# Attention, mixing MLP and gated output on one core: banks, copies and order of the first heads changed

## The chip, the cores and the metric

The kernel runs on one core of one Trainium2 chip. The metric is device microseconds of one execution, launch to end. A profiled execution also gives a trace. In it PE is the matrix engine (TensorE), DVE the vector engine, ACT the scalar engine, POOL GpSimd, SP the engine whose queue issues the DMAs here.

## What is computed

```python
# attn_out: 8 batches x 8 heads, 576 tokens, head size 64, block-causal mask (blocks of 64)
scores = scale * q @ k.T ; masked -> -1e9 ; p = exp(scores - max) ; p /= sum(p) + 1e-9
x = concat_heads(p @ v)                       # 8 x 576 x 512
h = x.T @ U @ V                               # mixing over tokens, rank 32
u = x + h.T
x = u + relu(u @ w_ch1) @ w_ch2               # 512 -> 2048 -> 512
gate = sigmoid(causal 5-tap convolution of x)
out = (gate * (x @ w_val)) @ w_out
```

U, V and the weights come as 64-bit floats; the kernel rebuilds single precision from their two words. Weights and most operands of the large products are split in a high and a low part, so that one product is three matmuls.

## The kernel before

**Stages.** A first stage runs the attention of batch 0 and of the first heads of batch 1 (ticks 0 to 11), with the mixing of batch 0, on an otherwise free PE. Then the MLP begins on groups of 512 tokens, sixteen steps each, and the remaining heads are cut in pieces that are dealt out between its matmuls (`gap`). At the end come the convolution, the gate and the last products.

**A tick.** `tick(n)` emits for head n the scores and for head e = n - 2 the values. For the first NQ = 18 heads (the early form) a tick has:

- two calls of `emit_q_bank`: each fills two PSUM banks with scores, one per head of the pair ("pS", from the pool `psum["a"]`), takes the row maxima on DVE ("rq", L415, and the negated maximum, L417 or L420) and the exponentials on ACT (L427, copies L425). Banks 0 and 1 of a pair come in the even tick, banks 2 and 3 in the odd one. All of it is at high priority.
- `mixing(2*e)`: steps of the token mixing of a pair of heads. In the first stage an even tick (from tick 4) has `mix_T`: PE turns the pair's normalised values `xt` ("pT", L646, L654), ACT and DVE split them. An odd tick (from tick 5) has `mix_G`: the product with U ("pG", L662), which goes by ACT (L664), DVE (L665), ACT (cast of g, L90) and DVE to `g`.
- `emit_pv(e, 0)` and `emit_pv(e, 1)`: the products of exponentials with values ("pPV", L586) for 128 and 448 tokens, each in a PSUM bank of `ps_p`; ACT copies the upper half of the bank to `xt` (L587) and the lower half, the sums of the exponentials, to `lt` (L588).
- `emit_est(e + 1)`, which for early heads is `emit_q_turn`: PE turns the exponentials of head e + 1 into four banks ("pE", L445), which ACT copies to the tile `e` (L446). It is at high priority.
- in an odd tick the normalisation of the pair: DVE turns `lt`, takes reciprocals, spreads them (L596 to L605), and POOL multiplies `xt` by them (L606).
- `mixing(2*e + 1)`: in an odd tick `mix_H`, the product with V ("pH", L685), the sum with `xt`, and the split into the MLP's `uh` and `ul`.

**What sets the order.** PE's instructions run in the order in which they are written. On the other engines a scheduler at build time orders by simulated readiness and by priority; each engine then works its queue in that order and waits at its head. In the first stage there are two PSUM pools of four banks: `ps_p`, from which pE, pPV, pT, pG and pH are taken in turn, and `psum["a"]`, from which pS is taken. A bank is taken again when the fourth allocation after it comes, and the writer waits until the earlier contents are read. From the first MLP step on both names are the same pool.

**Weights beside it.** Every twelfth `yield` of the stream in the first stage emits one conversion of a weight block (`conv`): a DMA of raw words, an absolute value on ACT ("wa", L119), four DVE operations (L121 to L142), a cast on ACT and a subtraction on POOL. The DMA of such a block is held back by a tiny DVE copy that reads the `xt` of the last emitted `emit_pv` (L553). After the first stage the remaining conversions are emitted two to a step, the first four together.

Of the kernel before, what the change touches and what calls it, by code (L numbers as in the profile page):

```python
# [8 lines left out]
F32 = mybir.dt.float32  # L9
# [8 lines left out]
P = 128  # L18
# [4 lines left out]
def attn_moe_gate_kernel(ctx: ExitStack, tc: tile.TileContext, q, k, v, U, V, w1, w2, wval, convw, wout, out):  # L23
    nc = tc.nc
    B, H, S, D = q.shape
# [46 lines left out]
    NQ = FIRST_SPLIT  # L72
# [14 lines left out]
    vec, act, pool, pe, sp = nc.vector, nc.scalar, nc.gpsimd, nc.tensor, nc.sync  # L87

    def hi_act(o, i):
        act.copy(o, i)  # L90
# [4 lines left out]
    def lo(eng, o, i, h):  # L95
        eng.tensor_tensor(o, i, f32(h), op=ALU.subtract)  # L96
# [63 lines left out]
    psum = {"a": first.enter_context(tc.tile_pool(name="ps0", bufs=8 - ABUF, space=PSUM, side="left"))}  # L160
# [39 lines left out]
    ps_p = att.enter_context(tc.tile_pool(name="psp", bufs=ABUF, space=PSUM, side="right"))  # L200
# [30 lines left out]
    def rot(tag, bufs=2, dtype=F32, n=S):  # L231
        return rot_p.tile([P, n], dtype, tag=tag, bufs=bufs, name=tag)
# [91 lines left out]
    def load_v(n):  # L324
        if not 0 <= n < NH:
            return
        vv = v[n // H, n % H]
        t = vstk[n % 2]
        sp.dma_start(out=t[:, 0:NK - 1, 0:D], in_=vv[0:S - D, :].rearrange("(i p) d -> p i d", p=P))
        sp.dma_start(out=t[D:P, NK - 1, 0:D], in_=vv[S - D:S, :])  # L330
# [3 lines left out]
    own = [slice(0, D), slice(D, P)]  # L334
# [13 lines left out]
    def kslice(j):  # L348
        return slice(q0[j], q0[j] + P) if q0[j] + P <= S else slice(S - P, S)
# [14 lines left out]
    def emit_s_piece(pn, i):  # L364
        heads = (2 * pn, 2 * pn + 1)
        if i == 0:
            for n in heads:
                stt[n] = [s_p.tile([P, w], F32, tag=f"s{h}", name=f"s{h}") for h, w in enumerate(sw)]
        todo, o = [], 0
        for j, a0, a1 in pieces[i]:  # L370
            todo.append((slice(a0, a1), kslice(j), o, True))
            o += a1 - a0
        j, a0, a1 = pieces[i][0]
        d = soff[j] + a0 - q0[j]
        for n, ps in zip(heads, beside(pn, todo)):
            act.copy(stt[n][half_of[j]][:, d:d + o], ps[:, 0:o])  # L376
# [54 lines left out]
    def emit_q_turn(n):  # L431

        eq = eqs.pop(n)
        for i, (half, c0, blocks) in enumerate(tbanks):
            if c0 == 0:
                e = e_p.tile([P, sw[half]], F32, tag=f"e{half}", name="e")
                est[n, half] = (e,)
            ps = ps_p.tile([P, 512], F32, tag="a", name="pE")
            o = c = D if i == 0 else 0
            todo = []  # L440
            for t, j in blocks:
                todo.append((t == NTT - 1, o if t < NTT - 1 else o - D, t, j))
                o += P if t < NTT - 1 else D
            for _, at, t, j in sorted(todo, key=lambda x: not x[0]):
                pe.transpose(ps[:, at:at + P], eq[t][:, kslice(j)], ident)  # L445
            act.copy(est[n, half][0][:, c0:c0 + o - c], ps[:, c:o])  # L446

    def emit_corners(n):
        for h, js in enumerate(((3, 0), (1, 2))):
            c0, c1 = (soff[j] // D for j in js)  # L450
            v_ = stt[n][h].rearrange("p (c w) -> p c w", w=D)
            pool.memset(v_[D:P, c0:c1 + 1:c1 - c0, :], MASKED)
        pool.memset(sv(n, NK - 1)[0:D], MASKED)
# [7 lines left out]
    def emit_max_a(n):  # L461
        m = rot("m", 1)
        vec.tensor_tensor(m[:, P:], sv(n, 0, P), sv(n, 1), op=ALU.max)
        for j in range(2, NK):
            x = vec.tensor_tensor(m[:, q0[j]:], m[:, q0[j]:], sv(n, j), op=ALU.max)
        noted(1, x)
        mxt[n] = m
# [30 lines left out]
    def emit_sub(n, half):  # L498
        mb = mbt[n]
        for j in parts[half]:  # L500
            noted(3, vec.tensor_tensor(sv(n, j), sv(n, j), mb[:, q0[j]:], op=ALU.subtract))  # L501
# [3 lines left out]
    def prep_v(n):  # L505

        if not FIRST_SPLIT <= n < NH:
            return
        t = vstk[n % 2]
        vlo[n] = late["v"].tile([P, NK, D], F32R, tag="vlo", name="vlo")  # L510
        if not vhi:
            vhi[0] = late["v"].tile([P, NK, P], F32R, tag="vhi", name="vhi")
            act.copy(vhi[0][:, :, D:P], t[:, :, D:P])
        v_, h_ = t[:, :, 0:D], vhi[0][:, :, 0:D]
        hi_act(h_, v_)
        lo(pool, vlo[n], v_, h_)
# [30 lines left out]
    last = [None]  # L547
# [7 lines left out]
    def emit_pv(n, c):  # L555
        b, h = divmod(n, H)
        pr, a = divmod(h, 2)
        if a == 0 and c == 0:
            xts[n // 2] = (late["x"] if n >= 3 * H and n // 2 % (NP + 2) == 0 else x_p).tile([P, S], F32, tag="xt", name="xt")
            lts[n // 2] = rot("lt", 1)  # L560
        xt, lt = xts[n // 2], lts[n // 2]
        last[0] = (own[a], xt[own[a]][0:1, 0:1])
        ps = ps_p.tile([P, 512], F32, tag="a", name="pPV")
        c0, c1 = ((0, P), (P, S))[c]
        split, whole = [], []
        for j in range(NK):
            a0 = max(c0, q0[j])
            if a0 >= c1:
                continue
            off = soff[j] - q0[j]  # L570
            rows = slice(0, P)
            o_, e_ = ps[:, a0 - c0:c1 - c0], slice(off + a0, off + c1)
            if n < FIRST_SPLIT:
                whole.append((o_, vstk[n % 2][rows, j, :], est[n, half_of[j]][0][rows, e_]))
            elif off + c1 <= WHOLE and half_of[j] == 0:
                whole.append((o_, vstk[n % 2][rows, j, :], est[n, 0][2][rows, e_]))
            else:
                eh, el, _, skip = est[n, half_of[j]]
                e_ = slice(off + a0 - skip, off + c1 - skip)
                for v_, m, t in ((vhi[0], P, eh), (vhi[0], P, el), (vlo[n], D, eh)):  # L580
                    split.append((o_[:m], v_[rows, j, 0:m], t[rows, e_]))
        todo = split + whole
        if len(todo) > 1:
            todo.append(todo.pop(1))
        for i, (o_, l_, r_) in enumerate(todo):
            pe.matmul(o_, l_, r_, start=(i == 0), stop=(i == len(todo) - 1))  # L586
        act.copy(xt[own[a], c0:c1], ps[0:D, 0:c1 - c0])  # L587
        act.copy(lt[own[a], c0:c1], ps[D:P, 0:c1 - c0])  # L588

    nrm = {}  # L590

# [105 lines left out]
    def tick(n, mixed, last=B * NP):  # L697


        e = n - DEPTH  # L700
        new, old = n < NH, 0 <= e < NH

        load_v(e + 1)
        for i in range(4):
            if n < NQ:
                if i % 2 == 0:
                    with tc.high_priority():
                        emit_q_bank(n // 2, 2 * (n % 2) + i // 2)
            elif new and n % 2 == 0:
                emit_s_piece(n // 2, i)  # L710
            if i == (0 if n % 2 else 3) and new and n >= NQ:
                emit_corners(n)
                emit_max_a(n)
            yield
        if new:
            if n >= NQ:
                emit_max_b(n)
            if n % 2 == 1:
                prep_t((n + 1) // 2)
        yield from mixing(2 * e, mixed, last)  # L720
        if new and n >= NQ:
            for _ in emit_max_c(n):
                pass
            emit_sub(n, 0)
            emit_sub(n, 1)
        if old:
            emit_pv(e, 0)
            yield
        if new and n >= NQ:
            emit_exp(n)  # L730
        if old:
            emit_pv(e, 1)
        prep_v(e + 1)
        emit_est(e + 1)
        if old:
            if e % 2 == 1:
                with tc.high_priority() if URG and e == H - 1 else ExitStack():
                    emit_norm_a(e // 2)
                    emit_norm_b(e // 2)
            yield  # L740
        yield from mixing(2 * e + 1, mixed, last)

    def mixing(at, first, last=B * NP):

        for step, delay in ((mix_H2, H0), (mix_G, G0), (mix_T, T0)) if last == NP else ((mix_H2, HPOS), (mix_G, GPOS), (mix_T, TPOS)):
            pn, off = divmod(at - delay, 4)
            if off == 0 and first <= pn < last:
                if URG and pn == NP - 1:
                    with tc.high_priority():
                        for _ in step(pn):  # L750
                            pass
                else:
                    yield from step(pn)
                yield step is mix_H2 and pn % NP == NP - 1
# [394 lines left out]
```

## Time and profile before

| | us |
|---|---|
| median of 3 runs | 1478.06 (1477.77 to 1481.87) |
| profiled execution | 1480.37 |
| its span | 1478.6 |
| PE busy | 1424.2 (96%) |
| DVE busy | 1034.4 (70%) |
| ACT busy | 724.5 (49%) |
| POOL busy | 293.1 (20%) |

A busy time counts what an engine's instructions took; their sum over an engine says little where stages have different limits, so the stretches are looked at one by one. The span is the profiled execution from its first to its last instruction; the execution's own time has 1.77 us more around it.

### The profile page before, as it was taken

What the parts mean: (1) busy time and instruction counts of PE and PEld (TensorE: products, weight loads), DVE (VectorE), ACT (ScalarE), POOL (GpSimd) and SP (SyncE); (2) the same over time, 40 slices, a digit from 0 to 9 for tenths busy, and PEclk for the clock granted to TensorE, in tenths of its full rate; (3) what the DMA queues carried; (4) which work ended last, traced back from release to release, by engine and by line L of the source; (5) the groups of instructions that cost most, each with busy time, mean ns of one, the idle gap of its engine ahead of it and who ended that gap; (6) DMA issues with size and microseconds to landing.
All of it is one profiled execution on the core that took longest, in us unless ns stands there. A gap on an engine that the chain in (4) does not pass through costs nothing.

```text
span 1478.6 us, 20133 instructions
## 1 busy us (share of the span) xinstructions
PE 1424.2 (96%) x6756; PEld 1098.7 (74%) x6756; DVE 1034.4 (70%) x2205; ACT 724.5 (49%) x1555; POOL 293.1 (20%) x410
## 2 busy tenths in 40 slices
PE   6777999999999999999999999999999999999999
PEld 4454667777777777777777777777888888878887
DVE  6677877777786888788778878877323326399991
ACT  4676655555555555455555564565222222344342
POOL 1123232211221112112211211121112100343310
PEclk7898999999999999999999999999999999999999
DMA  5345667433333434333433433332245433223311
GB/s 106 90 108 136 208 200 214 126 110 86 90 97 101 108 88 124 81 96 85 123 83 91 117 96 98 81 108 70 86 146 169 156 128 117 98 72 100 106 58 64
DMA packets 246288, 163.56 MB, mean 111 GB/s; under 512 B 197669, under 2 KB 212261, under 8 KB 246186
## 3 DMA queue, kind: packets, MB, share of 16 engines
q1 hardware_dynamic: 246186, 162.29, 38.8%
q8 instruction: 54, 0.88, 0.2%
q14 instruction: 48, 0.39, 0.1%
HBM read 134.98 MB, written 27.26 MB: 110 GB/s over the span
## 4 chain that ended last, share of the span: by engine, by line
PE 83%; DVE 6%; DMA 3%; ACT 3%; issue 2%; SPq 1%; POOL 1%; DVEq 0%; ACTq 0%; POOLq 0%
PE acc L868 25%; PE h L816 25%; PE pPV L586 8%; PE o L982 7%; PE val L958 6%; PE pS L361 6%; DMA raw<-in_moe_w_ch_dram 3%; DVE rq L415 2%; PE pG L662 1%; PE acc L861 1%; DVE wa L124 1%; PE pT L646 1%; ACT wa L119 1%; SPq L780 1%; SPq L318 1%
## 5 line engine op out<-in xcount | busy, mean ns | idle before, releaser
L868 PE MATMUL acc<-hh,w 128*128 128x512 f32 x1152 | 399.5, 400 | 0.0
L868 PEld LDWEIGHTS acc<-hh,w 128*128 128x128 f32 x1152 | 216.6, 188 | 68.6 <-issue 24.5
L816 PE MATMUL h<-uh,w1hi 128*128 128x512 f32 x576 | 237.1, 412 | 0.2
L816 PE MATMUL h<-ul,w1hi 128*128 128x512 f32 x576 | 226.4, 393 | 1.0 <-POOL ul L96 1.0
L816 PE MATMUL h<-uh,w1lo 128*128 128x512 f32 x576 | 226.8, 394 | 0.0
L868 PE MATMUL acc<-hl,w 128*128 128x512 f32 x576 | 225.6, 392 | 0.0
L845 DVE SCALAR_TENSOR_TENSOR hl<-h,hh 128x512 fp32r<-128x512 f32 x144 | 98.6, 685 | 143.5 <-ACT hh L844 142.3
L844 ACT ACTIVATE hh<-h 128x512 fp32r<-128x512 f32 x144 | 85.9, 597 | 176.1 <-PE h L816 170.2
L816 PEld LDWEIGHTS h<-uh,w1hi 128*128 128x128 f32 x576 | 109.2, 190 | 45.0 <-issue 21.8
L96 POOL TENSOR_TENSOR vlo<-vstk,vhi 128x320 fp32r<-128x320 f32 x46 | 43.2, 940 | 457.9 <-ACT vhi L90 417.6
L816 PEld LDWEIGHTS h<-uh,w1lo 128*128 128x128 f32 x576 | 108.9, 189 | 24.2
L816 PEld LDWEIGHTS h<-ul,w1hi 128*128 128x128 f32 x576 | 109.3, 190 | 20.2 <-POOL ul L96 1.3
L868 PEld LDWEIGHTS acc<-hl,w 128*128 128x128 f32 x576 | 108.6, 189 | 18.9 <-DVE hl L845 0.4
L376 ACT COPY s<-pS 128x320 f32<-128x320 f32 (+2 forms) x184 | 81.7, 496 | 73.6 <-PE pS L361 72.1
L940 DVE SCALAR_TENSOR_TENSOR gt<-yb,cw,gt 128x516 f32<-128x516 f32 (+1 forms) x144 | 115.2, 830 | 1.4
L523 ACT ACTIVATE s<-s 128x448 f32<-128x448 f32 x92 | 65.4, 711 | 93.4 <-DVE s L501 93.3
L501 DVE TENSOR_TENSOR s<-s,mb 128x64 f32<-128x64 f32 (+4 forms) x230 | 97.6, 489 | 0.5
L361 PE MATMUL pS<-tq,tk 64*128 64x320 f32 (+4 forms) x552 | 91.2, 429 | 0.8 <-ACT e L446 0.8
L96 POOL TENSOR_TENSOR yl<-yb,yh 128x512 fp32r<-128x512 f32 (+7 forms) x64 | 66.8, 1079 | 106.4 <-ACT yh L90 106.2
L96 DVE TENSOR_TENSOR el<-s,eh 128x448 fp32r<-128x448 f32 x92 | 69.5, 787 | 23.8 <-PE pPV L586 14.4
L96 POOL TENSOR_TENSOR ul<-xt,uh 128x512 fp32r<-128x512 f32 (+7 forms) x64 | 53.6, 848 | 108.8 <-ACT uh L90 108.7
L90 ACT CAST eh<-s 128x448 fp32r<-128x448 f32 x92 | 63.4, 697 | 13.4 <-PE pPV L586 13.4
(144 smaller groups left out, 2615.4 us busy)
## 6 DMA issues: line engine op xcount, KB each, us to landing
w<-w_s SPq DMA_DIRECT2D x144, 512.0 KB, 3.2
rawq<-in_q_dram SPq DMA_DIRECT2D x128, 72.0 KB, 2.7
rawk<-in_k_dram SPq DMA_DIRECT2D x128, 72.0 KB, 2.9
out_dram<-ot SPq DMA_DIRECT2D x35, 256.0 KB, 2.0
vstk<-in_v_dram SPq DMA_DIRECT2D x64, 128.0 KB, 2.7
raw<-in_moe_w_ch_dram SPq DMA_DIRECT2D x64, 128.0 KB, 3.1
raw<-in_moe_w_ch_dram SPq DMA_DIRECT2D x16, 512.0 KB, 3.7
w_s<-wo SPq DMA_DIRECT2D x16, 512.0 KB, 3.1
```

The costliest lines, as they stand in the source:

```text
L96: eng.tensor_tensor(o, i, f32(h), op=ALU.subtract)
L361: pe.matmul(ps[a][:, o:o + w], l_, r_, start=True, stop=True)
L376: act.copy(stt[n][half_of[j]][:, d:d + o], ps[:, 0:o])
L501: noted(3, vec.tensor_tensor(sv(n, j), sv(n, j), mb[:, q0[j]:], op=ALU.subtract))
L586: pe.matmul(o_, l_, r_, start=(i == 0), stop=(i == len(todo) - 1))
L816: pe.matmul(ps[:, 0:n], w[:, d, fs], x[:, d, 0:n], start=(d == 0 and i == 0), stop=(d == ND - 1 and i == 2))
L844: act.activation(hh[:, 0:n], ps[:, 0:n], AF.Relu)
L845: latest[0] = vec.scalar_tensor_tensor(hl[:, 0:n], ps[:, 0:n], 0.0, f32(hh[:, 0:n]), op0=ALU.max, op1=ALU.subtract)
L868: pe.matmul(acc[d][:, 0:n], w[:, wi, ds], x[:, 0:n], start=False, stop=(f == NF - 1 and i == 2))
L940: vec.scalar_tensor_tensor(gt[d][:, 0:gw], y[:, d, j:j + gw], cw[:, d, j:j + 1], gt[d][:, 0:gw], op0=ALU.mult, op1=ALU.add)
L958: pe.matmul(ps[:, 0:n], w[:, d, es], x[:, d, 0:n], start=(i == 0), stop=(i == 3 * ND - 1))
L982: pe.matmul(ps[:m, cs], x[:, e, a:a + m], w[:, e, cs], start=(i == 0), stop=(i == 3 * ND - 1))
```

## The change

Three edits, all for the early heads:

1. Of the four banks of turned exponentials of a head, the third and fourth come from the scores' pool `psum["a"]` and no longer from `ps_p`. From the first MLP step on the two are one pool, so this concerns the first stage.
2. The copies of `xt` and `lt` out of the values' bank are emitted at high priority.
3. `mixing(2*e)` (T or G) stands behind the two `emit_pv` calls, and ahead of the turning, where it stood ahead of both. The second `mixing` of a tick stays.

Edits 2 and 3 hold for ticks or heads under 18, so also for those dealt out in the first MLP group.

```diff
@@ emit_q_turn
-            ps = ps_p.tile([P, 512], F32, tag="a", name="pE")
+            ps = (ps_p if i < 2 else psum["a"]).tile([P, 512], F32, tag="a", name="pE")
@@ emit_pv
-        act.copy(xt[own[a], c0:c1], ps[0:D, 0:c1 - c0])
-        act.copy(lt[own[a], c0:c1], ps[D:P, 0:c1 - c0])
+        with tc.high_priority() if n < NQ else ExitStack():
+            act.copy(xt[own[a], c0:c1], ps[0:D, 0:c1 - c0])
+            act.copy(lt[own[a], c0:c1], ps[D:P, 0:c1 - c0])
@@ tick
-        yield from mixing(2 * e, mixed, last)
+        if n >= NQ:
+            yield from mixing(2 * e, mixed, last)
...
         if old:
             emit_pv(e, 1)
+        if n < NQ:
+            yield from mixing(2 * e, mixed, last)
         prep_v(e + 1)
         emit_est(e + 1)
```

## Rows read from the trace of the kernel before

**Rows 1.** Stretches: from:to, length, each engine's busy us, clock, DMA.

```profile
2.00:136.00 134.00, 97.31 (x498) 64.12 (x499) 90.90 (x274) 84.37 (x210) 22.29 (x26) 0.89 0.46 106
136.00:160.00 24.00, 20.18 (x72) 13.18 (x72) 20.27 (x37) 12.36 (x27) 9.65 (x8) 0.79 0.51 161
160.00:200.00 40.00, 37.02 (x174) 26.22 (x171) 32.44 (x72) 24.10 (x54) 12.28 (x11) 1.00 0.75 229
...
600.00:1000.00 400.00, 399.99 (x1972) 307.65 (x1971) 313.51 (x696) 221.75 (x469) 73.34 (x132) 1.00 0.37 97
```

**Rows 2.** Waits of PE, 0 to 136 us: total, times, longest.

```profile
PE pE L445 <- ACT lt L588: 14.2, 7, 5.4
PE pT L646 <- POOL xt L606: 10.1, 4, 3.3
PE pE L445 <- ACT s L427: 9.2, 5, 3.5
```

**Rows 3.** PE in order of time: start, length, instruction, idle before it.

```profile
39.68 0.47 PE L445 MATMUL pE<-ident,mb 128*128 128x128 f32 x1 [5.39 <-ACT lt L588]
...
90.81 2.00 PE L361 MATMUL pS<-tk,tq 64*128 64x384 f32 x12
95.11 0.66 PE L646 MATMUL pT<-ident,xt 128*128 128x128 f32 x4 [2.31 <-POOL xt L606]
...
95.71 2.98 PE L586 MATMUL pPV<-e,vstk 128*128 128x128 f32 x12
98.53 0.38 PE L445 MATMUL pE<-ident,mb 128*128 128x128 f32 x2
...
102.61 0.33 PE L445 MATMUL pE<-ident,mb 128*128 128x128 f32 x1 [2.61 <-ACT lt L588]
...
103.09 1.78 PE L361 MATMUL pS<-tk,tq 64*128 64x512 f32 x12
104.81 0.86 PE L662 MATMUL pG<-x,ust 128*128 128x256 f32 x5
105.50 2.98 PE L586 MATMUL pPV<-e,vstk 128*128 128x128 f32 x12
108.32 0.38 PE L445 MATMUL pE<-ident,m 128*128 128x128 f32 x2
...
111.17 0.33 PE L445 MATMUL pE<-ident,m 128*128 128x128 f32 x1 [1.01 <-ACT lt L588]
...
111.68 0.73 PE L685 MATMUL pH<-vst,g 128*128 128x512 f32 x2
112.34 2.00 PE L361 MATMUL pS<-tk,tq 64*128 64x384 f32 x12
...
137.31 1.25 PE L361 MATMUL pS<-tk,tq 64*128 64x384 f32 x8
```

**Rows 4.** ACT in order of time.

```profile
38.01 0.66 ACT L119 ACTIVATE wa<-raw 128x512 f32<-128x512 f32 x1 [3.65 <-DMA raw<-in_moe_w_ch_dram]
...
95.08 0.20 ACT L425 COPY m<-pS 128x64 f32<-128x64 f32 x1
...
100.81 0.66 ACT L119 ACTIVATE wa<-raw 128x512 f32<-128x512 f32 x1 [2.74 <-DMA raw<-in_moe_w_ch_dram]
...
102.59 1.68 ACT L446 COPY e<-pE 128x384 f32<-128x384 f32 x4
...
106.25 0.69 ACT L427 ACTIVATE s<-pS,rq 128x512 f32<-128x512 f32 x1 [0.21 <-DVE rq L420]
...
109.11 0.30 ACT L90 CAST g<-t 128x128 fp32r<-128x128 f32 x1
110.06 0.52 ACT L587 COPY xt<-pPV 64x448 f32<-64x448 f32 x1
...
146.21 0.22 ACT L425 COPY mb<-pS 128x64 f32<-128x64 f32 x1
```

**Rows 5.** POOL in order of time.

```profile
93.66 1.40 POOL L606 TENSOR_TENSOR xt<-xt,t 128x576 f32<-128x576 f32 x1
```

**Rows 6.** Stretches: the first and the last of four pairs of ticks.

```profile
49.17:71.36 22.19, 16.87 (x92) 11.26 (x91) 14.49 (x45) 15.39 (x40) 2.62 (x2) 0.92 0.50 123
...
112.34:135.75 23.41, 16.71 (x91) 11.27 (x90) 15.69 (x50) 16.23 (x42) 5.40 (x5) 0.93 0.47 116
```

## Prediction, made before the change was run

> **What bounds the kernel now.** I read the stretches first [rows 1]. From 160 us on PE is the bound: 37.0 of 40 us busy in its first 40 us, 399.99 of 400 later on. In the first stage it isn't: from 2 to 136 us PE is busy for 97.3 of 134 us, at a mean granted clock of 0.89 of its upper level, DVE for 90.9 and ACT for 84.4. No engine is full, so the stage is a chain that jumps between engines. Whatever the stage loses or gains at its end arrives at a PE that is then full to the end, so a microsecond there is nearly a microsecond of the run. The exception is the stretch from 136 to 160 us, where DVE is busy for 20.3 of 24 us with the conversions emitted at the seam.
>
> Next the waits of PE in that stage [rows 2]: 14.2 us in seven turnings (pE) that wait for the copy to `lt`, 10.1 us in four pT that wait for POOL's multiplication, and 9.2 us in five turnings that wait for an exponential. The change aims at the first two, 24.3 us together, and leaves the third as it is.
>
> Then PE's own order over one pair of ticks [rows 3]. Even tick from 90.81: scores for 2.0 us, idle for 2.31 until POOL has normalised `xt`, T, values from 95.71 to 98.53, turning, idle for 2.61 before its last bank, next scores at 103.09. Odd tick: scores, G at 104.81, values at 105.50, turning from 108.32, idle for 1.01, H at 111.68, scores at 112.34. So these are waits in the order written for PE, with ready work behind them.
>
> **The change part by part.**
>
> *T behind the values.* POOL's multiplication of that pair ran from 93.66 to 95.06 [rows 5], 4.25 us after the tick's first score; T stood ready for PE 2.0 us after it. The 2.82 us of values now come between (98.53 - 95.71, [rows 3]), so T comes 4.8 us after the tick's start and finds `xt` ready. The longest of the four waits is 3.3 us [rows 2], of which 0.5 would stay. The values need only the exponentials of the tick before; the copies of those end 1.2 us before the values in the pair shown (102.59 + 1.68 against 105.50, [rows 3, 4]). Gain 9.6 of 10.1 us. If the copies came later than the values are due, that would be the next wait; it is in the bank term below.
>
> *Copies at high priority, and two banks from the other pool.* The fourth turned bank waits for the bank of the second value product. Its copies stand on ACT behind other work: in both large cases shown ACT itself was waiting, at 38.01 and 100.81, for a DMA of raw weights (3.65 and 2.74 us, [rows 4]), and the copies stood behind that instruction. After the change the third and fourth banks take scores' banks whose exponentials are long done: the even tick's first bank is done at 95.28 (95.08 + 0.20, [rows 4]), 4.5 us after the tick's start; the odd one's at 106.94 (106.25 + 0.69), 3.9 us after. The third turned bank is due some 7 us after the start (2.0 + 2.8 + 0.6 of T or 0.7 of G + two banks of about 0.6). So 14.2 us go at this place. But the second pair of scores of the next tick now takes the banks of these turnings, and waits for ACT to copy them. Where ACT still stands at a raw block, the wait moves there, about one bank of scores (0.9 us, half of 1.78) further on. Bounds: all of the 14.2 kept if the copies of `xt`, `lt` and `e` come ahead of the weights' instruction; nothing but 0.9 us per wait, 6 us in seven, if they stay behind it. I take 8, nearer the lower end, since the DMA lands no earlier and the exponentials of the next tick stand behind it as well.
>
> *Scores behind the turned copies, without a DMA.* The four copies take 1.68 us [rows 4], so the last two end about 0.8 to 1.0 us after the last turning; the second scores are due 0.9 us after it in an odd tick, and behind H's 0.7 us as well in an even one. 0 to 0.8 us in five odd ticks; I take 0.3, 1.5 us in all.
>
> *First turnings behind the values.* In a tick with T the first two turned banks of `ps_p` take the values' banks, with only T's 0.6 us and one bank's 0.6 us between the last value and the second turning. The copies of `xt` and `lt` take about 1.05 us (two of 0.52, [rows 4]). 0 to 1 us if an exponential is ahead of them; I take 0.5 in four ticks, 2 us.
>
> *G behind the values.* G ended at 105.50 and its `g` was cast by 109.41 [rows 3, 4], 3.9 us later, with a DVE operation to come. H had 6.2 us. Now only the turning lies between, from 108.32 to 111.68, 3.4 us with its wait. So H waits 0 (if the queues are shorter then, because the maxima are past) to 1.2 us in four pairs. I take 0.6, 2.5 us.
>
> *Clock.* The first stage has a mean clock of 0.89, the last pair 0.93 [rows 1, 6], between the levels of 1.2 and 2.4 GHz, where the stretch from 160 us on, with less idle time, has 1.00. Shorter idle stretches may give back up to 3 us, or none; I take 1. At the seam nothing of this changes: DVE is full there in any case.
>
> *The ticks dealt out in the first MLP group* have the same order, but PE has other matmuls between: 3 of 40 us idle in [rows 1]. From -1 to +2 us; I take 0. No instruction or byte is added by any of the edits, and the conversions are emitted at the same yields; in one place (tick 10) that yield now lies behind the second value product and T, which holds one raw DMA back by up to 3 us.
>
> Sum: 9.6 + 8 - 1.5 - 2 - 2.5 + 1 = 12.6 us. The profiled execution (1480.37, span 1478.6) lies 2.3 us above the median of 1478.06; the difference is taken from the median: about 1466. Against the pairs [rows 6]: four pairs come from 22.2 and 23.4 us to about 19.5 each, with ACT at 16 and DVE at 15 us in one. That is full but possible.
>
> **The rivals.**
>
> *A. The exponentials become the chain (gain half lost).* ACT's queue is worked in order, and what is put ahead delays what is behind: in [rows 4] a copy of `xt` that could have run at 98.5 came after the DMA wait ending at 100.81. Copies at high priority that are placed ahead of the last exponentials of an odd tick hold those until the values are done and copied: 1.05 us in five odd ticks, while the wait for exponentials (9.2 us) grows and takes the place of a part of the waits removed. With the bank term at its lower end (6 for 8) the gain is 12.6 - 5.3 - 2 = 5.3 us, 1473. For it: ACT at 16.2 and DVE at 15.7 us of a pair. Against it: the copies take 1 us only, and the turnings have some slack in even ticks. The Trainium skill, page "PSUM — Partial Sum Buffer", section "Engine vs sequencer instructions", calls the queues of these engines strict FIFO; the copy's wait at 100.81 agrees, and by that rule every reordering here is an exchange.
>
> *B. Slower: the turning waits for the scores' banks.* The third and fourth banks now need the same tick's first scores to be through maxima and exponentials. That is 3.9 to 4.5 us after the tick's start now, 7 us are allowed. Where DVE serves conversions first it takes longer: of the scores begun at 137.31 the first bank was done at 146.43 [rows 3, 4], 9.1 us after. Beyond 7 us every tick waits by the excess, and each us costs 10 us in ten ticks; from 24.3 / 10, so 9.4 us after the start, the gain is eaten. At 10.5 us in every tick the run is 35 - 24 = 11 us slower, 1489. For it: the crowded seam. Against it: the maxima are at high priority, and in the pairs shown there are 2.5 us of slack.
>
> *C. No change.* The waits move to the copies of `e`, the scores and G's chain in full: the lower bank term (6), T's 9.6, less the upper ends of the other terms (4 for the scores, 4 for the turnings, 4.8 for G), and the dealt-out ticks at their worst (2): under 1 us of gain, 1477. For it: the DMA that held ACT is still there.
>
> **How the numbers follow.** Forecast, faster by 8 to 20 us: 0.55. A: 0.17. C: 0.16. B: 0.12. Under 0.3% (4.4 us) a measurement of this kernel can't be told from no change. A counts mostly as faster (0.13 of it): faster 0.68. C and the rest of A: same 0.20. B: slower 0.12. The forecast's own range is 1458 to 1470; with A and most of C the range is 1457 to 1477.
>
> **What would show it.** T without idle time for POOL; no turning that waits for `lt`, or under 3 us in all; the first MLP matmul (before at 135.75) some 12 us earlier, and the same distance kept to the end. New waits to look for: pS for copies of `e`, pH for `g`, pE for exponentials above 9.2 us. Wrong would be: pS idle behind copies of `e` for over 10 us, turnings that wait for the scores' banks, or a gain at 136 us that is gone by 300.

## The result and the profile after

The changed kernel takes 1491.33 us (median of 6, 1487.87 to 1491.99) where the kernel before takes 1479.12 beside it: ratio 1.0074, 95% interval 1.0057 to 1.0091. It is slower by 12 us by the medians and 11 by the ratio, where 12 us less were forecast. Its profiled execution took 1491.28 us, span 1489.6.

First the stretches of the changed kernel: the whole first stage (from 2 us to its first MLP matmul at 143.22, before at 135.75), and three short ones behind a pH. Columns as in [rows 1].

```profile
2.00:143.22 141.22, 104.34 (x498) 68.19 (x498) 94.48 (x279) 86.02 (x213) 22.64 (x27) 0.85 0.45 105
...
71.30:75.30 4.00, 4.00 (x15) 1.88 (x15) 2.44 (x10) 0.76 (x2) 2.65 (x3) 0.57 0.33 88
...
95.00:99.00 4.00, 4.00 (x15) 1.75 (x15) 2.61 (x10) 0.77 (x3) 2.59 (x3) 0.57 0.45 127
...
118.00:122.00 4.00, 4.00 (x15) 1.64 (x13) 2.47 (x10) 1.41 (x4) 2.18 (x3) 0.50 0.75 262
```

PE is idle for 141.22 - 104.34 = 36.9 us of the stage; before it was 134.0 - 97.3 = 36.7 [rows 1]. So as much idle time was made as was removed. PE's busy time for the same matmuls is 7 us longer, at a mean clock of 0.85 for 0.89. In these two executions that makes up the delay of 7.5 us at the first MLP matmul.

How much of these 7 us is the change's own is less sure. Of the stages below, the first is that of e17, whose instructions stand in the order of the kernel before up to the first MLP step, and the second that of e1, which differs from the changed kernel by G's place alone:

```profile
2.00:139.33 137.33, 102.42 (x498) 69.07 (x498) 91.53 (x275) 84.53 (x210) 22.22 (x26) 0.84 0.45 104
```

```profile
2.00:130.53 128.53, 100.34 (x497) 67.29 (x498) 91.95 (x276) 84.90 (x211) 22.33 (x26) 0.89 0.50 114
```

With the order of before, e17 is busy for 5 us more than the kernel before, at a clock of 0.84: so much differs from one execution to another. Nor is the growth the clock's alone: the scores alone are busy for 37.1 us in the changed kernel, 28.5 before, and e1 (34.6) and e2 (35.0), where H waits for nothing, have most of that already; e2 below shows why.

Against e1 the stage of the changed kernel is 12.7 us longer, by 8.7 us of idle time and 4.0 of busy time. That holds in other executions: with the first stage of e1 (e1, e9, e15, e18) PE is idle for 28.1 to 29.7 us and busy for 100.1 to 101.4, with that of the changed kernel (and e7) idle for 35.8 and 36.9, busy for 104.3 and 106.5.

Which waits went and came is in the waits of PE (0 to 150 us), to be laid beside [rows 2]:

```profile
PE pH L686 <- DVE g L96: 12.0, 4, 3.7
PE pS L361 <- ACT e L446: 8.4, 5, 4.1
PE pE L445 <- ACT s L427: 6.7, 3, 3.5
PE pE L445 <- ACT lt L589: 4.9, 5, 1.8
...
PE pE L445 <- ACT m L425: 1.8, 2, 0.9
```

No pT waits any more (before 10.1 us), and turnings wait 4.9 us for `lt` (before 14.2). In their place H waits 12.0 us for `g`, and scores wait 8.4 us for copies of `e`. Neither stands among the waits of the kernel before up to 136 us.

One pair of ticks in PE's order, answering to [rows 3]: G, turning, H, scores, values, T.

```profile
89.18 1.10 PE L663 MATMUL pG<-x,ust 128*128 128x256 f32 x5
90.11 0.38 PE L445 MATMUL pE<-ident,m 128*128 128x128 f32 x2
...
91.91 0.38 PE L445 MATMUL pE<-ident,s 128*128 128x128 f32 x2
94.93 0.50 PE L686 MATMUL pH<-vst,g 128*128 128x512 f32 x2 [2.63 <-DVE g L96]
95.36 3.66 PE L361 MATMUL pS<-tk,tq 64*128 64x384 f32 x12
98.94 3.08 PE L586 MATMUL pPV<-e,vstk 128*128 128x128 f32 x12
101.86 0.60 PE L647 MATMUL pT<-ident,xt 128*128 128x128 f32 x4
```

ACT and then DVE in the same time:

```profile
91.50 0.53 ACT L589 COPY lt<-pPV 64x448 f32<-64x448 f32 x1
92.06 0.73 ACT L427 ACTIVATE s<-pS,rq 128x128 f32<-128x128 f32 x2
92.68 0.27 ACT L665 COPY t<-pG 128x128 f32<-128x128 f32 x1
92.83 1.37 ACT L446 COPY e<-pE 128x384 f32<-128x384 f32 x3
94.04 0.35 ACT L90 CAST g<-t 128x128 fp32r<-128x128 f32 x1
```

```profile
92.98 0.29 DVE L666 TENSOR_TENSOR t<-pG,t 128x128 f32<-128x128 f32 x1
...
94.50 0.28 DVE L96 TENSOR_TENSOR g<-t,g 32x128 fp32r<-32x128 f32 x1
```

The reader is to see two things. G ends at 90.28 (89.18 + 1.10), but ACT takes it up at 92.68, behind the copies of `xt` and `lt` and two exponentials, and the cast of `g` stands behind three copies of `e`: `g` is done at 94.78, 4.5 us after G ends. PE has only the turning between, and is done with that at 92.29. And the scores behind the wait take 3.66 us where they took 2.00 [rows 3]: in that stretch the granted clock is 0.57, near the lower of the two levels.

The rest of the 11 us comes between the first MLP matmul and the second token group: its first accumulation (`acc<-uh,identr`) starts at 334.01 us, before at 323.12. From there to the end both take 1155.5 us, as do all kernels below within 1.2 us. So three marks tell where a kernel gains or loses (one profiled execution each):

| | first MLP matmul | first accumulation | second group | span |
|---|---|---|---|---|
| before | 135.8 | 153.1 | 323.1 | 1478.6 |
| changed | 143.2 | 160.5 | 334.0 | 1489.6 |
| e1 all but G's move | 130.5 | 139.9 | 308.1 | 1463.5 |
| e2 banks alone | 135.3 | 150.7 | 323.4 | 1478.5 |
| e3 order alone | 144.0 | 159.5 | 331.3 | 1486.8 |
| e5 T's move alone | 134.7 | 145.8 | 317.7 | 1474.4 |
| e13 G's move alone | 140.9 | 155.9 | 337.3 | 1493.5 |
| e16 G's move, first stage | 142.4 | 157.3 | 330.4 | 1486.5 |
| e17 G's move, later ticks | 139.3 | 155.8 | 335.8 | 1491.6 |

The marks carry some 3 to 4 us of scatter, as e17's first one shows (3.6 us behind the kernel before, in the same order), and e17's profiled execution is 6 us above its median. So the times below decide. One execution of e18 took 2785.16 us and is left out of its ratio.

### The profile page after: what moved, and what is told of

Read it like the earlier page. It is cut to its first block, busy times and chain, and to the rows that moved or that the text cites. A ratio compares the mean times of both kernels' runs of the same rounds, so it can differ in the third digit from the quotient of the medians.

```text
span 1489.6 us, 20130 instructions
## 1 busy us (share of the span) xinstructions
PE 1434.3 (96%) x6756; PEld 1104.4 (74%) x6756; DVE 1038.2 (70%) x2205; ACT 724.7 (49%) x1555; POOL 292.3 (20%) x410
## 4 chain that ended last, share of the span: by engine, by line
PE 86%; DVE 4%; ACT 4%; DMA 3%; SPq 1%; issue 1%; POOL 0%; DVEq 0%; ACTq 0%
PE acc L872 26%; PE h L820 26%; PE pPV L586 9%; PE pS L361 7%; PE o L986 7%; PE val L962 6%; DMA raw<-in_moe_w_ch_dram 2%; PE pG L663 1%; PE acc L865 1%; DVE rq L415 1%; ACT e L446 1%; PE pT L647 1%; ACT wa L119 1%; SPq L318 1%; DVE wa L124 1%
## 5 line engine op out<-in xcount | busy, mean ns | idle before, releaser
L501 DVE TENSOR_TENSOR s<-s,mb 128x64 f32<-128x64 f32 (+4 forms) x230 | 97.3, 487 | 0.5
L96 DVE TENSOR_TENSOR el<-s,eh 128x448 fp32r<-128x448 f32 x92 | 70.2, 795 | 23.2 <-PE pPV L586 14.2
L361 PE MATMUL pS<-tk,tq 64*128 64x512 f32 (+4 forms) x216 | 57.3, 548 | 17.6 <-ACT e L446 8.4
```

Source lines behind the costliest of these rows:

```text
L361: pe.matmul(ps[a][:, o:o + w], l_, r_, start=True, stop=True)
```

## The experiments

Each was timed in five rounds beside the kernel before; ratios are to that, with 95% intervals.

**e1. G back ahead of the values, all else changed.**

```diff
-        if n >= NQ:
+        if n >= NQ or e % 2:
             yield from mixing(2 * e, mixed, last)
...
-        if n < NQ:
+        if n < NQ and e % 2 == 0:
             yield from mixing(2 * e, mixed, last)
```

> All three edits, but G (the mixing of odd ticks) stays ahead of the values; only the mixing of even ticks moves. Theory G (the price is G's chain to H, 12.0 us of waits of pH and the lower clock behind them): those waits go to under 1 us, the scores after H are back at about 2 us, the first MLP matmul comes at 128 to 133 us, total 1472 to 1478. Theory B (the price is the bank sharing, 8.4 us of waits of pS for copies of e): waits of pS stay at 8 us or more and the total at 1484 or above.

Measured: 1465.53 us, 0.9890 (0.9877 to 0.9904): 25.8 us under the changed kernel, 15 under before, and below what was expected. No pH waits; the waits of its first stage are

```profile
PE pE L445 <- ACT s L427: 10.0, 4, 3.5
PE pS L361 <- ACT e L446: 6.8, 5, 4.0
PE pE L445 <- ACT lt L589: 5.8, 4, 2.0
...
PE pT L647 <- POOL xt L607: 0.6, 1, 0.6
```

So the waits of pS, which theory B blamed, stay at 6.8 us in a kernel that is the fastest of all. Theory B falls. Theory G stands as to what makes the change slow; why the kernel is faster still than it said is taken up below, and stays open.

**e2. The banks alone.** The diff is the first hunk of the change.

> Before with the first edit alone (two of the four turned banks from the scores' pool). Theory G: 14.2 us of waits for lt fall, part comes back as pS behind copies of e, total 1472 to 1479, not slower. Theory B: waits of pS for e of 8 us, DVE later by as much, total 1484 to 1488.

Measured: 1479.58 us, 0.9990 (0.9981 to 0.9999). In its first stage no turning waits for `lt`, and pS waits 8.6 us for copies of `e`: an exchange, as the prediction had it at its lower bound. Not the cause.

```profile
PE pS L361 <- ACT e L446: 8.6, 5, 5.0
```

There is a price that no wait shows. PE's idle time in the stage fell to 29.2 us (36.7 before), but its busy time rose to 104.1 (97.1). The scores of the stage have nearly all of that, 35.0 us for 28.5. Those at 70.19 take 3.73 us where they took 2.00 [rows 3], with the granted clock at 1.00.

```profile
70.19 3.73 PE L361 MATMUL pS<-tk,tq 64*128 64x384 f32 x12
```

```profile
70.30 0.74 ACT L427 ACTIVATE s<-pS,rq 128x128 f32<-128x128 f32 x2
```

In the scores at 90.81 of [rows 3] the matmuls of the two heads start two by two, 0.01 us apart. Here the second head's first one starts at 71.09, 0.9 us after the first head's, when ACT has read the last scores out of an earlier bank (71.04), and no two of the six start together. Sharing the banks takes the two heads apart.

**e3. The order alone.** The diff is the third hunk.

> Before with the third edit alone (T and G behind the values). Theory G: waits of pH for g of 10 us or more, scores after H at half clock, waits for lt stay, total 1486 to 1494. Theory B: pT waits gone and nothing lost, total 1466 to 1472.

Measured: 1488.90 us, 1.0052 (1.0039 to 1.0065), in the range of theory G; pH waits 7.5 us, less than the 10 that were expected, and turnings wait 14.5 us for `lt`.

**e7. All edits, the order moved only in the first stage.**

```diff
-        if n >= NQ:
+        if n >= NQ or last != NP:
...
-        if n < NQ:
+        if n < NQ and last == NP:
```

> All three edits, but the order moves only in the first stage; in the ticks dealt out between MLP matmuls it stays. Theory S (3.5 of the 11 us are lost after the first stage by the same order there): total 1487 to 1488, first MLP matmul at 143 as in the changed kernel. Rival (what is lost there comes from the later start and the queue order as the scheduler happens to set it): total within 1.5 us of 1491, or off in either direction without relation.

Measured: 1483.67 us, 1.0015 (1.0005 to 1.0024), 7.7 us under the changed kernel: more than theory S asked, and it doesn't rule out the rival, which left the size open. That the order in the later ticks costs is settled by e17 and e18 below.

**e5. T's move alone** (e1's order, without the other edits).

> Before with the third edit for even ticks alone: T behind the values, G where it was, no bank from the scores' pool. Theory N (the banks only exchange waits for lt against waits of pS, as alone, where they were worth 1 us): within 3 us of the kernel with all but G's move (1465.5), so 1463 to 1469, waits of turnings for lt 8 us or more, waits of pS for e under 1. Rival P (the banks pay once T no longer stands ahead of the values, because T's and the values' banks meet in one pool): 1471 to 1477.

Measured: 1476.28 us, 0.9966 (0.9953 to 0.9979): rival P. The 10.1 us of T's waits are gone, but turnings wait 17.2 us for `lt` there (14.2 before), and PE's idle time in the stage is 34.0 us (36.7): most of it came back elsewhere. Banks alone are worth 1 us and T's move alone 3 to 5 (by medians and by ratio), but both together 12 (e11).

**e8. G's cast on DVE, in the changed kernel.**

```diff
-        hi_act(g, g32)
+        (hi_vec if pn < NP else hi_act)(g, g32)
```

> The changed kernel with the cast of g on DVE, not on ACT, in the first stage: G's chain goes once through ACT's queue, not twice. Theory Q (H waits because g's two ACT instructions stand behind exponentials and copies of e in ACT's queue): waits of pH fall from 12.0 us to 4 to 9, total 1481 to 1489. Rival D (the chain's own length is the price, whatever the queue): waits of pH stay at 11 to 13 us, total within 2 us of 1491.

Measured: 1484.12 us, 1.0023 (1.0009 to 1.0038), 7 us under the changed kernel. Up to 128 us pH waits 5.3 us in three, where it was 9.1; the fourth waits 5.0, where it was 2.9. In all that is 10.3 us for 12.0, not the 4 to 9 that theory Q expected, though the time is in its range. Three of the waits are shorter for the way past ACT's queue. But turnings wait 11.4 us for `lt` (4.9 in the changed kernel), and the first MLP matmul comes at 141.6 us, only 1.7 earlier. Most of the 7 us are gained behind it; by what was not followed.

```profile
68.62 0.51 PE L686 MATMUL pH<-vst,g 128*128 128x512 f32 x2 [1.43 <-DVE g L96]
69.05 2.00 PE L361 MATMUL pS<-tk,tq 64*128 64x384 f32 x12
...
114.12 0.50 PE L686 MATMUL pH<-vst,g 128*128 128x512 f32 x2 [2.47 <-DVE g L96]
114.55 3.23 PE L361 MATMUL pS<-tk,tq 64*128 64x384 f32 x12
```

In one and the same kernel the scores behind the shorter wait run in 2.00 us, those behind the longer in 3.23, at a granted clock of 1.00 and 0.59.

**e9. e1, the order moved only in the first stage.** (T behind the values if `last == NP`.)

> All but G's move (1465.5), and the order moves only in the first stage, so H stays ahead of the values in the ticks between MLP matmuls. Theory S (the order in those ticks costs by itself, as the 7.6 us between 1491.3 and 1483.7 suggest): 1459 to 1463. Rival (that difference came from how the seam at the first MLP step falls, not from the order later on): within 2 us of 1465.5, and the same first MLP matmul at 130 us.

Measured: 1469.34 us, 0.9924 (0.9909 to 0.9938). Neither expectation came true. Theory S in this general form falls: where G stays ahead, moving the later mixing (there it is H) behind the values gains some 4 us.

**e10. The changed kernel, H one tick later.**

```diff
-    H0 = 7
+    H0 = 9
```

> The changed kernel with H one tick later (H0 9 for 7), so that G stays behind the values and its chain has a whole tick before H. Theory G (the price is the short way from G to H): waits of pH under 1 us, scores behind it at full clock, total 1464 to 1474 (the last pair's H comes without a tick before it, 3 us at most). Rival (G behind the values costs in another way, as in the exponentials that ACT delays): 1480 or above.

Measured: 1477.72 us, 0.9985 (0.9971 to 1.0000). Three of four waits of pH are gone, the fourth is 1.7 us, the first MLP matmul is back at 133.9 us; but the total misses the expected range. The later ticks still have G behind the values, and e18, with the same later ticks, has nearly the same time. That fits, but e10 with those ticks put back was not run.

**e13. G's move alone**, on the kernel before.

```diff
-        yield from mixing(2 * e, mixed, last)
+        if n >= NQ or e % 2 == 0:
+            yield from mixing(2 * e, mixed, last)
...
             emit_pv(e, 1)
+        if n < NQ and e % 2:
+            yield from mixing(2 * e, mixed, last)
```

> Before with one thing changed: in ticks of the early form with odd e the mixing (G) stands behind the values; T, banks and copies as before. Theory G (G's place is what made the changed kernel slow): pH waits for g 5 us or more, scores behind H slower, total 1486 to 1496 (the price of G with the banks and T moved was 25.8 us; without them there is other idle time for it to hide in). Rival (it is slow only together with T's move or the banks, which crowd ACT): within 4 us of before.

Measured: 1496.21 us, 1.0105 (1.0091 to 1.0119): 16 us slower, more than the whole change. This alone is enough to make the change slow, and without it (e1) the change is fast. Its PE:

```profile
63.22 1.11 PE L662 MATMUL pG<-x,ust 128*128 128x256 f32 x5
...
71.05 0.85 PE L685 MATMUL pH<-vst,g 128*128 128x512 f32 x2 [2.51 <-DVE g L96]
71.83 3.79 PE L361 MATMUL pS<-tk,tq 64*128 64x384 f32 x12
...
93.13 0.50 PE L685 MATMUL pH<-vst,g 128*128 128x512 f32 x2 [1.06 <-DVE g L96]
93.56 3.63 PE L361 MATMUL pS<-tk,tq 64*128 64x384 f32 x12
```

**e11. e1 without the priority of the copies.**

> T behind the values and the banks, without the priority of the copies. Theory C0 (the priority is worth nothing: in the first stage every queue has the same order with and without it): within 2 us of 1465.5. Rival: the few copies of lt that it moves in the first MLP steps carry part of the gain, total 1468 to 1474.

Measured: 1468.62 us, 0.9917 (0.9904 to 0.9931), 3 us above e1 by the medians and 4 by the ratios, in the rival's range; the two intervals touch. The order of ACT's queue in the first stage is the same with and without the priority; only two places at and behind the first MLP steps differ. So the priority is worth 0 to 4 us. By itself in the kernel before it leaves the order of every engine as it is in the built program; that kernel was not run.

**e14. Two conversions at the first MLP step, not four**, on the kernel before, **and e15**, the same on e1.

```diff
-                conv(2 * LEAD if f == 0 else 2)
+                conv(2)
```

> Before with two weight conversions emitted at the first MLP step, not four (the others follow one step later each; none is left out). Theory Z (the 17.3 us from the first MLP matmul to the first accumulation are long because four conversions stand ahead of the maxima in DVE's queue, and PE idles into the lower clock): that stretch 10 to 14 us, total 1471 to 1476. Rival Y (the conversions' own rate bounds the whole first group, so what the seam gives is taken back before the second group): stretch shorter, total within 2 us of before.

> All but G's move, with two conversions at the first MLP step as well. Theory Z: its stretch of 9.3 us is already without the stall, so within 2 us of 1465.5; rival Y: slower by the later conversions, 1467 to 1471. A version faster than 1465.5 is possible only if the conversions still hold the maxima after 139 us: 1461 to 1464.

Measured: e14 1478.64 us, 0.9985 (0.9974 to 0.9995); e15 1467.93 us, 0.9916 (0.9902 to 0.9929). In e14 the stretch from the first MLP matmul to the first accumulation is 13.8 us, not 17.3, and the second group starts at 323.7, as before: rival Y. e15 is in the range of rival Y too. No gain that can be told from none in either.

**e16, e17. G's move alone in the first stage, or alone in the later ticks; e18: the changed kernel with G back in the first stage alone.** (e13's condition with `last == NP`, with `last != NP`; e1's with `last == NP`.)

> Before with G behind the values in the first stage alone. G behind the values everywhere cost 16.0 us (1496.2 against 1480.2): 5.1 us by the first MLP matmul and the rest later. If the place of G in the first stage is the cause of both, by the state in which it leaves the queues at the first MLP step: 12 us or more slower. If the later ticks carry the rest by themselves: 3 to 8 us slower.

> Before with G behind the values only in the ticks that are dealt out between MLP matmuls (three of them have odd e). If these carry the rest of the 16.0 us by themselves: 7 to 12 us slower, first MLP matmul at 135 to 136 us as before. If the first stage is the cause: within 3 us of before.

> The changed kernel with G back ahead of the values in the first stage alone; in the later ticks all stays moved. First MLP matmul at 129 to 132 us. If the later G's cost by themselves: 1472 to 1478. If only the first stage counts: 1464 to 1468, as with G back everywhere (1465.5).

Measured: e16 1486.25 us, 1.0036 (1.0022 to 1.0050); e17 1487.16 us, 1.0044 (1.0027 to 1.0060); e18 1477.13 us, 0.9974 (0.9961 to 0.9987). Both places cost by themselves, 5 and 6 us (0.36 and 0.44% of 1481), which leaves 4 to 5 of e13's 16 us to the two together. e17 is under the 7 to 12 us that were expected if the later ticks carried all the rest; e18's time is in the range for later G's that cost by themselves. Beside the other edits both cost more: e18 is e1 with the three later G's behind the values, and 11 us slower; the changed kernel has the first stage's G's there as well, and is 14 us slower again.

## Why the prediction was wrong

The step that failed is *G behind the values*. It was priced at 0 to 1.2 us a pair, 2.5 us in all. H waited 12.0 us in four pairs, and G's place costs 16 us alone (e13) and 26 us beside the other edits (e1 against the changed kernel). Three things were wrong in it.

*The cover.* The turning between G and H was taken as 3.4 us "with its wait", from 108.32 to 111.68 [rows 3]. But that wait was one which the other edits remove. Without it the turning takes 90.11 to 92.29, 2.2 us. The gain at one place was the cover at another, and it was counted twice. From the end of G to the end of the last matmul ahead of H it is 1.6, 2.0, 1.6 and 4.4 us in the four pairs, before 6.1 to 8.1. That is not the whole of it: in e13, where turnings still wait, it is 3.6 to 4.2 us in the first three pairs, as the prediction took it, and H waits 6.4 us in these three all the same.

*The chain.* It was read from one pair, and the queues might be shorter, it said, when the maxima are past. From the end of G (105.67 in that pair; 105.50 is where the values start) to the end of `g` the four pairs before take 5.8, 4.1, 4.1 and 5.4 us, and the pair shown is one of the two short ones. Behind the values it is 4.2, 4.5, 5.2 and 7.1 us, in e13 6.7, 4.5, 6.3 and 9.0. So it didn't become shorter, and it is longer than what covers it in each of these pairs. ACT's queue has much to do there: copies of `xt` and `lt`, the last exponentials and the copies of `e` all fall due in those microseconds, and G's two ACT instructions stand among them. With one of the two on DVE (e8) the chain takes 2.9, 2.9, 4.5 and 6.9 us.

*The clock.* The prediction gave it +1 us, since idle time would shrink. Idle time stayed the same, and the scores behind three of the waits of H took 3.6 to 3.8 us for 2.0, at a granted clock of 0.50 to 0.54: 5 us together. The same scores took 2.00 us in each of three executions with the order of before (before, e14, e17). Against e1 only 2.7 of the 5 us are G's, as the same scores take 8.4 us there, two of the three at a clock of 1.00, with the two heads' matmuls not all together.

The term for the later ticks (0, -1 to +2 us) was also mis-sized. G's place there costs some 6 us by itself (e17) and 11 beside the other edits (e18 against e1). H's place there gives some 4 back (e9 against e1), and e7 against the changed kernel has the two together, 7.7. Which wait carries that was not settled. e17's later part shows waits of pS for ACT's copies of earlier scores (4.0 and 2.8 us, before 2.7 in one) and of values for exponentials (3.1, before 1.6), but no one of them was taken away by itself.

The other steps: T's waits are gone, as said (10.1 to 0). The waits for `lt` fell by 9.3 us and 8.4 came back at pS, against 8 kept: the lower bound was right for the waits when the banks came alone (e2), but only 1 us of time came of it, since scores of the two heads no longer ran together, a price that the sum does not have. With T moved the banks are worth more: e11 is 7.7 us faster than e5; why is not shown.

e1 is the changed kernel without the failed step, and its 1465.53 is what was forecast (1466), but that is luck, since the way there was not the forecast one: its first MLP matmul comes only 5.2 us earlier, and 8.0 us more are gained between that and the first accumulation, where the prediction said that nothing would change. There its stretch against that of before (whose row comes second):

```profile
130.53:139.87 9.34, 9.09 (x40) 5.69 (x39) 8.90 (x19) 5.28 (x12) 6.34 (x5) 1.00 0.51 168
```

```profile
135.75:153.07 17.32, 13.49 (x38) 8.05 (x39) 14.75 (x29) 8.40 (x18) 7.03 (x6) 0.70 0.57 182
```

For the same matmuls DVE has 8.9 us of work in place of 14.8, and the clock is 1.00, not 0.70. In e1 DVE begins the maxima of the scores at 132.08 at 133.46; before, those of the scores at 137.31 began at 142.71, behind conversions, and the scores at 145.90 waited 2.7 us for ACT's copy of an earlier bank. But e14 shortened this stretch and gained nothing, so the stretch by itself is not the gain; how e1 keeps it to 308 us is open.

Of the rivals: A did not come, the waits for exponentials fell from 9.2 to 6.7 us. C had the direction of the exchange, but no loss. B came near with its number (1489) and not with its mechanism: turnings waited 1.8 us in two for the scores' banks, not in every tick.

## What to carry to other kernels

When a step is moved later, take its own product along to the instruction that needs it, and measure the way that is left with the waits that the same change removes taken out. A step whose result passes a full queue twice belongs ahead of the work that hides it. Price a group of edits also one by one: here one part of an edit turned a gain of 15 us into a loss of 11. And look at busy time beside idle time when a wait is taken away: the banks took 7 us of idle time out of the stage and put 7 us of busy time in (e2).

## What the runs showed of the hardware

In the changed kernel the stretch behind a wait of 3.70 us had a granted clock of 0.50, the lower level of 1.2 GHz, behind 2.63 us 0.57; in e8 scores behind 1.43 us ran at 1.00 and at the speed of [rows 3]. The wait just before is not the whole of it: in e13 scores behind a wait of 1.06 us took 3.63 us at 0.54, with 0.55 and 0.58 us of idle time in the turning ahead of it.

The idle time of a whole stage does not tell its clock: with the same order up to the first MLP step, the kernel before and e17 were idle for 36.7 and 34.9 us, and their mean clocks were 0.89 and 0.84.

Matmuls can take longer at the upper level too. In e1 the scores at 66.76 took 3.49 us with the granted clock at 1.00: there the matmuls of the two heads, which use 64 rows each, ran one behind the other (the second head's from 67.42 on), where those of [rows 3] started together and took 2.00.
